# A list scheduler inside the kernel, 4096-wide feed-forward groups, and zeros sent through TensorE during the first keys

## The chip, the core and the metric

The kernel runs on one core of one Trainium2 chip. The metric is the time of one execution in microseconds of device time. The profile's span, from the first to the last instruction, is about 2 us shorter. In the profile's lines PE is TensorE (matrix multiply), PEld its weight loads, DVE is VectorE, ACT is ScalarE, POOL is GpSimd and SP is the engine that issues most DMAs. A run is called slow when it is over 1.5% above the fastest of the same kernel; only fast runs are compared unless the text says otherwise. The sets of experiments ran on four different chips, so each ratio below is to the runs of the kernel before in the same set.

## The reference, cut to what matters

```python
# attention with sketched features: batch 4, heads 4, 1088 positions, head_dim 32, r = 8
a = S1 x ; b = S2 x                       # 8 numbers each per position
phi(x) = outer(a, b)                      # 64 features
kv = sum over s of phi(k) v ; z = sum over s of phi(k)
x = (phi(q) kv) / (phi(q) z + 1e-6)       # 4352 tokens x 128
# feed-forward, d_ff = 2048
h = x @ w_in
P = a0 + a1 h + a2 h^2 + a3 h^3
Q = 1 + |b0| |h| + |b1| h^2
out = (P / (Q + 1e-6)) @ w_out            # float32
```

## The kernel before: what the change and the argument touch

Work is cut into eight chunks of 512 tokens and one of 256. A chunk first needs the keys of its batch (`kv`), then its queries, which give the transposed activations `xT`, and then goes through the feed-forward part. There the 2048 hidden columns of 512 tokens are taken in four groups; a group's tiles are 128 partitions x 2048 elements.

```python
def moe_chunk(xT, W, gf, fill, store_rows):          # gf = 4
    for g in range(ng):
        hb = ...                                      # bf16 copy of h
        for s in range(0, gf, nsub):
            h_ps = hps.tile([128, 1024], FP, name="h_ps")
            ... matmul(h_ps, lhsT=w_in_sb[...], rhs=xT)          # L287
            nc.scalar.copy(out=hb[...], in_=h_ps)                # L289
        m = |hb|                 # bitwise and, VectorE            L291
        u = m * b1 + b0          # VectorE                         L294
        u = u * m                # VectorE                         L296
        L = Ln(u + 1)            # ScalarE                         L298
        r = Exp(-L)              # ScalarE: 1/Q                    L300
        p = hb * a3 + a2         # VectorE                         L302
        p = p * hb               # VectorE                         L304
        p = p + a1               # VectorE                         L305
        p = p * hb               # VectorE                         L306
        y = p * r                # VectorE                         L308
        ... matmul(out_ps, w_out * a0, r), then matmul(out_ps, w_out, y)   # L313
        for f in fill[g::ng]:    # a piece of the next chunk's queries and keys
            f()
# ... cut: key_features, kv_add, query_pieces (p_qT, p_pair(0), p_pair(1), p_xT), output
```

So a group has eight wide VectorE instructions in two chains: the denominator chain (`m`, `u`, `u`, then Ln and Exp on ScalarE) and the numerator chain (four instructions, then the product with `r`). In `p_pair` one pair of heads goes through matmul, ScalarE copy, matmul, VectorE product `q_pT`, matmul `nd`, VectorE division, and only then the second pair starts. The text gives an order of issue, but the framework may move instructions of each engine by its own priorities.

## Time and profile before

| | before |
|---|---|
| time, median of the first 4 runs | 363.36 us (361.62 to 364.05) |
| span of the profiled run | 359.8 us |
| start, until the first `m` on VectorE | 44.43 us |
| middle, first `m` to the end of the last `y` | 307.11 us, VectorE busy 280.65 |
| tail | 8.3 us |

TensorE's busy share is not a good measure of how near it is to its limit: the Trainium skill, "Perfetto Trace Analysis", section "Identifying the Most-Contended Engine", says so, because matmuls are pipelined, and this case agrees, since the same number of recorded matmuls (1004) fills 270 us of the middle here and 248 us in the changed kernel.

Two stretches of the same kernel, from the windows view. The columns are the stretch, its length, and the busy us (and count) of each engine:

```profile
core 0: us, PE busy (x) PEld busy (x) DVE busy (x) ACT busy (x) POOL busy (x), PEclk, DMA share, GB/s
0.00:44.43 44.43, 35.13 (x111) 24.08 (x112) 11.06 (x33) 8.38 (x14) 6.60 (x27) 1.00 0.58 175
44.43:351.54 307.11, 269.98 (x1004) 136.17 (x1020) 280.65 (x379) 219.28 (x195) 2.75 (x2) 0.94 0.03 11
```

In the start VectorE does 11 us of work in 44. In the middle it is idle for 26.5 us. Its largest wait, from the view of its waits (us in total, times, longest), is for `hb`; the longest of the five is the first `m`, so 12.7 us of it fall into the middle:

```profile
DVE m L291 <- ACT hb L289: 20.2, 5, 7.5
```

Four lines from the timeline, start and duration first, show the start of the kernel and, for comparison, the same matmul later:

```profile
22.94 2.07 PE L231 MATMUL w_ps<-qT,Srep_158 64*128 64x512 f32 x2 [0.67 <-ACT qT L225]
29.48 2.07 PE L231 MATMUL w_ps<-qT,Srep_158 64*128 64x512 f32 x2
44.43 0.69 DVE L291 TENSOR_SCALAR m<-hb 128x2048 int16<-128x2048 int16 x1 [7.45 <-ACT hb L289]
46.71 1.12 PE L231 MATMUL w_ps<-qT,Srep_158 64*128 64x512 f32 x2
```

One logical matmul in float32 is recorded as two. It takes 2.07 us at 23 us and 1.12 us at 47 us: TensorE runs at half rate in the start, although the PEclk column says 1.00 there. The Trainium skill, "TensorE: Matmul & The Clock Gate", Part 1, says that an idle array is gated to half rate and released by some 3.4 us of sustained work. The halved duration agrees with the two rates. The release does not come as stated: in the record TensorE works nearly without a gap from 10 to 20 us, and stays at half rate.

```profile
10.00:20.00 10.00, 9.53 (x44) 9.22 (x43) 2.93 (x10) 1.30 (x4) 0.00 (x0) 1.00 0.84 261
12.67 3.20 PE L188 MATMUL kv_ps<-v_aug,k_p 128*128 128x66 f32 x14
```

The same 14 matmuls take 1.78 us at 64.71 us.

Finally the order of VectorE in the middle, from its timeline:

```profile
87.23 1.22 DVE L306 TENSOR_TENSOR p<-p,hb 128x2048 bf16<-128x2048 bf16 x1
88.37 0.81 DVE L294 TENSOR_SCALAR u<-m,b_abs 128x2048 bf16<-128x2048 bf16 x1
89.09 0.81 DVE L302 TENSOR_SCALAR p<-hb,a_sb 128x2048 bf16<-128x2048 bf16 x1
89.81 1.22 DVE L296 TENSOR_TENSOR u<-u,m 128x2048 bf16<-128x2048 bf16 x1
90.95 1.22 DVE L304 TENSOR_TENSOR p<-p,hb 128x2048 bf16<-128x2048 bf16 x1
```

The two chains alternate, so that no instruction needs its neighbour's result. Each starts 0.08 to 0.09 us before the recorded end of the one in front (88.37 + 0.81 = 89.18, the next starts at 89.09).

### The profile page before, as it was taken

How to read it: one execution, taken by the hardware profiler on the slowest of the kernel's cores; microseconds unless marked ns; L12 is line 12 of the kernel's file. 1: busy time of each engine (PE TensorE's matmuls, PEld its weight loads, DVE VectorE, ACT ScalarE, POOL GpSimd, SP SyncE). 2: the span in 40 equal slices, each digit the busy share in tenths (PEclk: the TensorE clock that was granted, in tenths of full speed). 3: DMA queues.
4: the chain of work that ended last, by engine and by line, in shares of the span. 5: the costliest groups of instructions: out<-in, count | busy, mean ns of one | idle time of the engine just before them, and what ended most of it. 6: DMA issues, size and time to landing. Idle time of an engine off the chain costs nothing.

```text
span 359.8 us, 3085 instructions
## 1 busy us (share of the span) xinstructions
PE 307.7 (86%) x1124; PEld 161.5 (45%) x1141; DVE 291.7 (81%) x411; ACT 228.4 (63%) x211; POOL 9.3 (3%) x29
## 2 busy tenths in 40 slices
PE   3988999899869998899598999996899689949652
PEld 2855435654323455544244466443444234426431
DVE  1323199999997998899889998999889984998790
ACT  2110387648947885679649964896499556972960
POOL 4011000030000000000000000000000000000000
PEclk9999999999998999999989999999899959996965
DMA  5791300200000200000000000000000000000000
GB/s 146 240 311 47 118 0 1 60 0 1 29 0 2 87 0 2 1 29 0 2 0 0 29 2 0 29 0 3 0 0 30 0 2 29 0 0 0 2 29 16
DMA packets 12127, 11.22 MB, mean 31 GB/s; under 512 B 4048, under 2 KB 10448, under 8 KB 11984
## 3 DMA queue, kind: packets, MB, share of 16 engines
q1 hardware_dynamic: 12112, 11.02, 9.9%
q8 instruction: 9, 0.15, 0.2%
q14 instruction: 6, 0.05, 0.0%
HBM read 8.79 MB, written 2.23 MB: 31 GB/s over the span
## 4 chain that ended last, share of the span: by engine, by line
PE 55%; DVE 21%; ACT 19%; issue 2%; DMA 1%; SPq 0%; DVEq 0%; ACTq 0%
PE h_ps L287 22%; PE out_ps L313 12%; ACT L L298 8%; PE kv_ps L188 5%; ACT hb L289 5%; PE w_ps L231 4%; DVE y L308 4%; PE w_ps L236 4%; DVE u L296 3%; PE w_ps L243 3%; DVE p L306 3%; DVE p L304 2%; PE w_ps L171 2%; DVE u L294 2%; DVE m L291 2%
## 5 line engine op out<-in xcount | busy, mean ns | idle before, releaser
L287 PE MATMUL h_ps<-xT,w_in_sb 128*128 128x512 f32 (+1 forms) x288 | 137.0, 608 | 4.2 <-ACT xT L260 2.4
L289 ACT CAST hb<-h_ps 128x1024 bf16<-128x1024 f32 x68 | 67.9, 1016 | 42.9 <-PE h_ps L287 42.9
L287 PEld LDWEIGHTS h_ps<-xT,w_in_sb 128*128 128x128 f32 x288 | 55.2, 203 | 60.3 <-issue 38.7
L298 ACT ACTIVATE L<-u,one_ap 128x2048 f32<-128x2048 bf16 x34 | 68.3, 2010 | 8.8 <-DVE u L296 8.6
L313 PE MATMUL out_ps<-y,w_out_b 128*128 128x512 bf16 (+1 forms) x139 | 39.5, 408 | 4.9 <-DVE y L308 4.5
L306 DVE TENSOR_TENSOR p<-p,hb 128x2048 bf16<-128x2048 bf16 x34 | 41.4, 1218 | 0.2
L304 DVE TENSOR_TENSOR p<-p,hb 128x2048 bf16<-128x2048 bf16 x34 | 41.4, 1218 | 0.2
L296 DVE TENSOR_TENSOR u<-u,m 128x2048 bf16<-128x2048 bf16 x34 | 41.3, 1214 | 0.0
L291 DVE TENSOR_SCALAR m<-hb 128x2048 int16<-128x2048 int16 x34 | 23.2, 683 | 20.3 <-ACT hb L289 20.2
L313 PEld LDWEIGHTS <-w_out_a_291 128*128 128x128 bf16 x144 | 14.5, 102 | 42.3 <-issue 34.3
L313 PEld LDWEIGHTS <-w_out_b 128*128 128x128 bf16 x144 | 15.1, 109 | 29.4 <-issue 20.8
L302 DVE TENSOR_SCALAR p<-hb,a_sb 128x2048 bf16<-128x2048 bf16 x34 | 27.3, 804 | 0.0
L294 DVE TENSOR_SCALAR u<-m,b_abs 128x2048 bf16<-128x2048 bf16 x34 | 27.1, 798 | 0.0
L305 DVE TENSOR_SCALAR p<-p,a_sb 128x2048 bf16<-128x2048 bf16 x34 | 26.2, 770 | 0.3
L243 PEld LDWEIGHTS w_ps<-kv_dup,q_pT 128*128 128x128 f32 x128 | 17.4, 208 | 15.4 <-DVE q_pT L239 14.8
L243 PE MATMUL w_ps<-kv_dup,q_pT 128*128 128x66 f32 x128 | 18.9, 296 | 4.7 <-DVE q_pT L239 4.7
L188 PEld LDWEIGHTS kv_ps<-v_aug,k_p 128*128 128x128 f32 x128 | 19.3, 227 | 6.1 <-issue 2.9
L231 PE MATMUL w_ps<-qT,Srep_158 64*128 64x512 f32 (+1 forms) x36 | 21.3, 672 | 0.7 <-ACT qT L225 0.7
L188 PE MATMUL kv_ps<-v_aug,k_p 128*128 128x66 f32 x128 | 20.2, 309 | 0.7 <-DVE k_p L180 0.7
L236 PE MATMUL w_ps<-qT,Srep_162 64*128 64x512 f32 (+1 forms) x36 | 20.2, 643 | 0.3 <-ACT A_sb L234 0.3
L234 ACT COPY A_sb<-w_ps 128x512 f32<-128x512 f32 (+1 forms) x18 | 10.1, 562 | 13.2 <-PE w_ps L231 13.1
L239 DVE TENSOR_TENSOR q_pT<-A_sb,w_ps 128x512 f32<-128x512 f32 (+1 forms) x18 | 11.7, 653 | 7.2 <-PE w_ps L236 7.0
(167 smaller groups left out, 304.1 us busy)
## 6 DMA issues: line engine op xcount, KB each, us to landing
in_k_dram<-in_k_dram SPq DMA_DIRECT2D x4, 512.0 KB, 3.9
in_v_dram<-in_v_dram SPq DMA_DIRECT2D x4, 512.0 KB, 5.2
in_q_dram<-in_q_dram SPq DMA_DIRECT2D x4, 512.0 KB, 4.3
out_dram<-oT SPq DMA_DIRECT2D x8, 256.0 KB, 2.0
w_in_sb<-in_moe_w_in_dram SPq DMA_DIRECT2D x1, 1024.0 KB, 8.3
k_rem<-in_k_dram SPq DMA_DIRECT2D x4, 32.0 KB, 4.1
v_rem<-in_v_dram SPq DMA_DIRECT2D x4, 32.0 KB, 2.2
q_rem<-in_q_dram SPq DMA_DIRECT2D x4, 32.0 KB, 5.8
```

Source lines behind the costliest of these rows:

```text
L188: nc.tensor.matmul(kv_tiles[b][:, hp * 66:(hp + 1) * 66], lhsT=k_rows[:, hp * 128:(hp + 1) * 128], rhs=v_rows[:, 2 * hp:2 * hp + 2, :], st ...
L231: nc.tensor.matmul(A_ps[:, :W], lhsT=Srep[0][rows].rearrange("p g f -> p (g f)"), rhs=st["qT"][rows, :W], start=True, stop=True)
L236: nc.tensor.matmul(B_ps[:, :W], lhsT=Srep[1][rows].rearrange("p g f -> p (g f)"), rhs=st["qT"][rows, :W], start=True, stop=True)
L243: nc.tensor.matmul(nd_ps[r0:r1, i * 66:(i + 1) * 66], lhsT=q_pT[:, i * 128 + r0:i * 128 + r1], rhs=kv_of(b, i, hp), start=True, stop=True)
L287: nc.tensor.matmul(h_ps[:, i * W:(i + 1) * W], lhsT=w_in_sb[:, fi * 128:(fi + 1) * 128], rhs=xT[:, :W], start=True, stop=True)
L289: nc.scalar.copy(out=hb[:, s * W:(s + nsub) * W], in_=h_ps)
L294: nc.vector.tensor_scalar(out=u[:, :GW], in0=m[:, :GW], scalar1=b_abs[:, 1:2], scalar2=b_abs[:, 0:1], op0=AX.mult, op1=AX.add)
L296: nc.vector.tensor_mul(out=u[:, :GW], in0=u[:, :GW], in1=m[:, :GW])
L298: nc.scalar.activation(out=L[:, :GW], in_=u[:, :GW], func=ACT.Ln, bias=one_ap)
L304: nc.vector.tensor_mul(out=p[:, :GW], in0=p[:, :GW], in1=hb[:, :GW])
L306: nc.vector.tensor_mul(out=p[:, :GW], in0=p[:, :GW], in1=hb[:, :GW])
L313: nc.tensor.matmul(out_ps[:, :W], lhsT=W_terms[t][:, fi, :], rhs=ys[t][:, i * W:(i + 1) * W], start=(g == 0 and t == 0 and i == 0), stop=( ...
```

## The change

The intent is to feed VectorE without gaps: decide the order of every engine's queue in the kernel, halve the number of wide VectorE instructions, and raise TensorE's clock early. The long diff is cut to its core.

```diff
+class Plan:                       # every step: engine, estimated ns, what it follows, rank, buffers taken and given
+    HOP = 190
+    def issue(self):
+        while todo:                # of the steps that are ready, the one that can start first, then by rank
+            ...
+            key = (t, s["rank"], s["n"])
+        for s in sorted(done, key=lambda s: (s["start"], s["n"])):
+            s["fn"]()
-    GF = 4
+    GF = 8                        # groups of 4096 elements
+    LW = 2048                     # Ln and Exp stay 2048 wide
+    FR = 1.45                     # feed-forward matmuls ranked 1.45 groups ahead
+    FIRST = [4, 4, 8]             # group sizes of the first chunk
+    LAST = [8, 4, 4]              # and of the last, 256-token chunk (2048, 1024, 1024)
+    ctx.enter_context(tc.manual_schedule())
+    BUFS = dict(xT=3, hb=3, m=1, u=2, r=2, y=2, L=2, h_ps=2, ...)
+    def warm(n):
+        for _ in range(n):
+            nc.tensor.matmul(warm_ps[0], lhsT=zeros[:, :128], rhs=zeros, start=True, stop=True)
+    # warm(8) first; then 1 or 2 of them among the transposes, projections and kv
+    # matmuls of the first keys, and in the first chunk's queries
+    c_w = plan.add("DVE", 2500, weights, after=[ld["ab"], ld["wo"]], rank=-0.25, give=["L"])
+    # queries: both pairs of heads advance together, step by step, instead of one after the other
+    d1 = plan.add("DVE", ts, d_abs, after=[he, c_b], rank=g - 0.5, take=["m"])
+    d2 = plan.add("DVE", ts + 100, d_lin, after=[d1], rank=g - 0.5, take=["u"])
+    d3 = plan.add("DVE", tt, d_mul, after=[d2], rank=g - 0.5, give=["m"])
+    ... Ln, Exp and the r half of the projection, 2048 columns at a time ...
+    p = plan.add("DVE", ts + 100, n_first, after=[he, ld["ab"]], rank=g - 0.3, take=["y"])
+    p = plan.add("DVE", tt, n_mul, after=[p], rank=g - 0.3)
+    p = plan.add("DVE", ts + 50, n_add, after=[p], rank=g - 0.3)
+    p = plan.add("DVE", tt, n_mul, after=[p], rank=g - 0.3, give=["hb"])
+    p = plan.add("DVE", tt, n_over, after=[p, e], rank=g + 0.55)
# ... cut: all helpers turned into steps; the numerator is now formed in y, without a tile p
```

## The prediction

> **What bounds the kernel now.** The span is 359.8 us (median time 364.03). Windows view, three stages:
>
> 1. Start, 0 to 44.4 us: VectorE is nearly empty (about 11 us busy); it waits 7.5 us for the first `hb`. The timeline shows one serial chain (keys, `kv`, queries, `xT`, first `h_ps`), with the PE clock low: a pair of `L231` matmuls takes 2.07 us here and 1.05 us later; the first `h_ps` pair about 1.7 us against 0.86 us later (the granted-clock row's 1.0 contradicts that). The Trainium skill, "TensorE: Matmul & The Clock Gate", Part 1, says an idle array runs at half rate until about 3.4 us of sustained work; the halved durations agree.
> 2. Middle, 44.4 to 351.6 us (307.2 us): VectorE busy 280.7 us (91%), ACT 219, PE about 270 by the record, but by full-clock spacings (0.86 us per `h_ps` matmul, 0.22 us per `out_ps` matmul) I estimate 250 us of real PE work. VectorE is the bound; 26 us of idle remain.
> 3. Tail, 8.3 us from the last `y` to the end.
>
> **What the change does.**
>
> - Zeros through PE: 8 matmuls before the keys and some 30 among them, at 0.22 us warm about 7 us of extra PE work. If the clock rises, the pre-`h_ps` chain halves in its PE parts. By hand: `kv` ready about 17.5 us (was 22.5), `xT` about 25 (was 38.3), first VectorE group instruction about 30 us instead of 44.4. Gain 14 us.
> - 4096-wide groups: 34 groups become 20, about 112 fewer wide VectorE instructions. At 77 to 187 ns of start cost each that looks like 12 us; I expect almost none. In before, instructions of two chains alternate (`m`, `p`, `u`, `p`, ...) and start 0.61, 0.72, 1.14 us apart although they last 0.68, 0.81, 1.22: independent neighbours overlap. Where neighbours depend on each other (the last group), the starts are 0.85 and 1.25 us apart. The new order runs each chain straight through (`m`,`u`,`u`; then `y`,`y`,`y`,`y`), five of eight instructions dependent, costing 0.11 us each. Per 4096 columns: before 2 x 7.28 = 14.56 us, after about 14.27. The whole is about 247 us either way. Ln and Exp stay 2048 wide.
> - Scheduler order: orders come from durations close to the trace's, and feed-forward matmuls are hoisted 1.45 groups ahead. VectorE efficiency in the middle should rise from 91% to about 96.5%: (247 + 32 of small operations)/0.965 = 289 us, a gain of 18 us.
> - Tail: last group 1024 wide, 4 matmuls instead of 8: about 7.5 us.
>
> **Sum.** 30 + 289 + 7.5 = 326.5 us span; time about 2 us over the span, as before: **328 us**, 8 in 10 between 315 and 344. Faster by over 2%: 0.95; within 2%: 0.04; slower: 0.01.
>
> **What would show each step right or wrong.** First `m` at 27 to 34 us, and early `w_ps` pairs near 1.05 us rather than 2 us; wide VectorE instructions averaging about 1.22, 1.33 and 2.29 us, total VectorE busy near 285 to 292, hardly down; VectorE idle in the middle below 15 us; PE clock dips rarer; tail 7 to 8 us.
>
> **What would make it wrong.** The zeros may fail to raise or hold the clock between the short matmuls (start 35 to 40 us). The fixed order stalls an in-order engine where real times differ from the planned ones (up to 345). Dependent neighbours may cost less at 4096 (down to 318).

## More of the kernel before

From the page of the kernel before, the busy times of the engines and the chain that ended last (the chain of waits), by engine and then by line:

```profile
PE 307.7 (86%) x1124; PEld 161.5 (45%) x1141; DVE 291.7 (81%) x411; ACT 228.4 (63%) x211; POOL 9.3 (3%) x29
PE 55%; DVE 21%; ACT 19%; issue 2%; DMA 1%; SPq 0%; DVEq 0%; ACTq 0%
PE h_ps L287 22%; PE out_ps L313 12%; ACT L L298 8%; PE kv_ps L188 5%; ACT hb L289 5%; PE w_ps L231 4%; DVE y L308 4%; PE w_ps L236 4%; DVE u L296 3%; PE w_ps L243 3%; DVE p L306 3%; DVE p L304 2%; PE w_ps L171 2%; DVE u L294 2%; DVE m L291 2%
```

No engine owns the chain: it passes between PE, VectorE and ScalarE.

## The result, and the profile after

The changed kernel takes 324.28 us (median of 4 runs, 323.23 to 326.02) against 363.36 us. The ratio of the fast runs is 0.8936, with a 95% interval from 0.8882 to 0.8990. Such a ratio is the mean time of one kernel's fast runs over that of the other's fast runs of the same rounds, so it is not quite the ratio of the medians. The result is correct. The profiled run has a span of 323.9 us.

The same parts of the page after the change:

```profile
PE 280.0 (86%) x1153; PEld 150.0 (46%) x1172; DVE 286.5 (88%) x300; ACT 228.4 (71%) x213; POOL 8.7 (3%) x29
DVE 77%; PE 13%; DMA 5%; issue 1%; SPq 1%; ACT 1%; DVEq 0%
DVE y L503 22%; DVE u L486 11%; DVE y L510 10%; DVE y L499 6%; DVE u L482 6%; DVE y L506 6%; PE h_ps L466 6%; DVE m L476 5%; DMA L<-in_moe_w_out_dram 3%; DVE q_pT L398 3%; DVE k_p L314 2%; PE out_ps L517 2%; PE w_ps L405 2%; DMA v_sb<-in_v_dram 2%; PE w_ps L389 2%; DVE x_sb L417 2%
```

VectorE's work hardly fell (291.7 to 286.5 us) although it has 111 instructions fewer. What changed is who owns the chain: VectorE, with 77% in place of 21%. The windows view of the two stretches:

```profile
0.00:35.77 35.77, 30.78 (x144) 18.84 (x147) 11.36 (x34) 9.55 (x16) 6.62 (x27) 0.95 0.74 217
35.77:316.47 280.70, 247.57 (x1004) 130.46 (x1020) 275.15 (x267) 218.07 (x195) 2.09 (x2) 0.97 0.04 12
```

The profiled runs are the fastest of the four before and the slowest of the four after, so their spans differ by less than the medians (39.1 us). The 35.9 us between the spans are 8.7 us in the start (44.43 to 35.77), 26.4 us in the middle (307.11 to 280.70) and 0.8 us in the tail (8.26 to 7.43). Of the 26.4 us, 5.5 are less VectorE work and 20.9 less VectorE idle time (26.5 to 5.6). The wait for `hb` is left at the first `m` alone:

```profile
DVE m L476 <- ACT hb L472: 7.5, 1, 7.5
```

VectorE's order in the middle, after:

```profile
219.71 1.22 DVE L476 TENSOR_SCALAR m<-hb 128x4096 int16<-128x4096 int16 x1
220.97 1.34 DVE L482 TENSOR_SCALAR u<-m,b_abs 128x4096 bf16<-128x4096 bf16 x1
222.35 2.29 DVE L486 TENSOR_TENSOR u<-u,m 128x4096 bf16<-128x4096 bf16 x1
224.56 2.29 DVE L510 TENSOR_TENSOR y<-y,r 128x4096 bf16<-128x4096 bf16 x1
226.76 1.34 DVE L499 TENSOR_SCALAR y<-hb,a_sb 128x4096 bf16<-128x4096 bf16 x1
228.14 2.29 DVE L503 TENSOR_TENSOR y<-y,hb 128x4096 bf16<-128x4096 bf16 x1
```

Each chain now runs straight through. Where an instruction needs its neighbour's result it starts 0.04 us after the neighbour's end (219.71 + 1.22 = 220.93, next 220.97); where it does not (224.56 after 222.35 + 2.29 = 224.64), 0.08 us before. So a dependence costs 0.12 us here, and a group has five.

The start did not go as predicted. From the timeline after the change, VectorE and then TensorE:

```profile
20.54 1.29 DVE L258 TENSOR_SCALAR w_out_108<-L,a_sb 128x2048 bf16<-128x2048 f32 x1 [2.27 <-DMA L<-in_moe_w_out_dram]
21.75 1.22 DVE L259 CAST w_out_109<-L 128x2048 bf16<-128x2048 f32 x1
23.00 1.29 DVE L398 TENSOR_TENSOR q_pT<-A_sb,w_ps 128x512 f32<-128x512 f32 x2
35.77 0.69 DVE L476 TENSOR_SCALAR m<-hb 128x2048 int16<-128x2048 int16 x1 [7.49 <-ACT hb L472]
23.74 1.18 PE L405 MATMUL w_ps<-kv_dup,q_pT 128*128 128x66 f32 x8 [2.71 <-DVE q_pT L398]
25.57 1.81 PE L405 MATMUL w_ps<-kv_dup,q_pT 128*128 128x66 f32 x8
```

The two conversions of `w_out` stand in VectorE's queue in front of the first `q_pT`. They wait for their load, and TensorE waits 2.71 us behind them. After that gap its second set of `L405` matmuls takes 1.81 us. Up to the gap the start had gone as predicted: `kv` was ready at 16.96 us (17.5 predicted), and two early pairs of `w_ps` matmuls took 1.87 us together.

### The profile page after: what moved, and what is told of

It reads as the page before. It is cut to its first block, busy times and chain, and to the rows that moved or that the text cites. A ratio compares the mean times of both kernels' runs of the same rounds, so it can differ in the third digit from the quotient of the medians.

```text
span 323.9 us, 3027 instructions
## 1 busy us (share of the span) xinstructions
PE 280.0 (86%) x1153; PEld 150.0 (46%) x1172; DVE 286.5 (88%) x300; ACT 228.4 (71%) x213; POOL 8.7 (3%) x29
## 4 chain that ended last, share of the span: by engine, by line
DVE 77%; PE 13%; DMA 5%; issue 1%; SPq 1%; ACT 1%; DVEq 0%
DVE y L503 22%; DVE u L486 11%; DVE y L510 10%; DVE y L499 6%; DVE u L482 6%; DVE y L506 6%; PE h_ps L466 6%; DVE m L476 5%; DMA L<-in_moe_w_out_dram 3%; DVE q_pT L398 3%; DVE k_p L314 2%; PE out_ps L517 2%; PE w_ps L405 2%; DMA v_sb<-in_v_dram 2%; PE w_ps L389 2%; DVE x_sb L417 2%
## 5 line engine op out<-in xcount | busy, mean ns | idle before, releaser
L490 ACT ACTIVATE L<-u,one_ap 128x2048 f32<-128x2048 bf16 (+1 forms) x35 | 68.4, 1954 | 18.1 <-DVE u L486 18.1
L503 DVE TENSOR_TENSOR y<-y,hb 128x4096 bf16<-128x4096 bf16 (+2 forms) x40 | 78.9, 1972 | 1.2
L495 ACT ACTIVATE r<-L 128x2048 bf16<-128x2048 f32 (+1 forms) x35 | 65.4, 1870 | 0.4
L517 PE MATMUL out_ps<-r,w_out_108 128*128 128x512 bf16 (+1 forms) x139 | 35.6, 378 | 11.6 <-ACT r L495 11.2
L517 PE MATMUL out_ps<-y,w_out_109 128*128 128x512 bf16 (+1 forms) x132 | 34.4, 389 | 10.7 <-DVE y L510 9.9
L486 DVE TENSOR_TENSOR u<-u,m 128x4096 bf16<-128x4096 bf16 (+2 forms) x20 | 39.4, 1971 | 0.6
L510 DVE TENSOR_TENSOR y<-y,r 128x4096 bf16<-128x4096 bf16 (+2 forms) x20 | 39.3, 1965 | 0.1
L517 PEld LDWEIGHTS <-w_out_109 128*128 128x128 bf16 x144 | 14.4, 104 | 32.1 <-issue 21.7
L482 DVE TENSOR_SCALAR u<-m,b_abs 128x4096 bf16<-128x4096 bf16 (+2 forms) x20 | 23.7, 1185 | 0.6
L499 DVE TENSOR_SCALAR y<-hb,a_sb 128x4096 bf16<-128x4096 bf16 (+2 forms) x20 | 23.6, 1181 | 0.0
L405 PE MATMUL w_ps<-kv_dup,q_pT 128*128 128x66 f32 x128 | 16.9, 288 | 5.4 <-DVE q_pT L398 5.4
L405 PEld LDWEIGHTS w_ps<-kv_dup,q_pT 128*128 128x128 f32 x128 | 16.6, 204 | 9.7 <-DVE q_pT L398 7.7
L389 PE MATMUL w_ps<-qT,Srep_106 64*128 64x512 f32 (+1 forms) x36 | 16.9, 615 | 0.1
```

What stands on the lines that cost most here:

```text
L405: nc.tensor.matmul(nd_ps[r0:r1, i * 66:(i + 1) * 66], lhsT=T["q_pT", n, hp][:, i * 128 + r0:i * 128 + r1], rhs=kv_of(b, i, hp), start=True ...
L482: nc.vector.tensor_scalar(out=T["u", g][:, :gw], in0=T["m", g][:, :gw], scalar1=b_abs[:, 1:2], scalar2=b_abs[:, 0:1], op0=AX.mult, op1=AX.add)
L486: nc.vector.tensor_mul(out=T["u", g][:, :gw], in0=T["u", g][:, :gw], in1=T["m", g][:, :gw])
L490: nc.scalar.activation(out=T["L", g, l0][:, :lw], in_=T["u", g][:, l0:l0 + lw], func=ACT.Ln, bias=one_ap)
L495: nc.scalar.activation(out=T["r", g][:, l0:l0 + lw], in_=T["L", g, l0][:, :lw], func=ACT.Exp, scale=-1.0)
L499: nc.vector.tensor_scalar(out=T["y", g][:, :gw], in0=T["hb", g][:, :gw], scalar1=a_sb[:, 3:4], scalar2=a_sb[:, 2:3], op0=AX.mult, op1=AX.add)
```

## The experiments

All kernels gave correct results. The first `m` and the last `y` of each are read from its timeline, the busy times between them from its windows view.

| kernel | time, median us | ratio to before | first `m` | middle | VectorE busy in it |
|---|---|---|---|---|---|
| before | 363.36 | | 44.43 | 307.11 | 280.65 |
| changed | 324.28 | 0.894 | 35.77 | 280.70 | 275.15 |
| no_zeros | 331.14 | 0.914 | 42.82 | 282.29 | 275.36 |
| narrow | 356.92 | 0.982 | 38.17 | 309.60 | 295.19 |
| narrow_alt | 331.22 | 0.919 | 36.50 | 285.26 | 281.08 |
| before_wide | 450.58 | 1.244 | 48.88 | 390.77 | 267.73 |
| framework_order | 328.18 | 0.906 | 40.22 | 278.90 | 266.69 |
| weights_late | 320.47 | 0.882 | 31.38 | 279.55 | 274.96 |
| alternate | 324.46 | 0.892 | (slow profile) | | |
| both | 321.89 | 0.885 | 33.41 | 279.09 | 268.01 |
| lagged | 343.68 | 0.948 | (slow profile) | | |
| lagged_fr | 332.50 | 0.918 | 33.23 | 289.92 | 269.85 |
| before_zeros | 372.43 | 1.017 | (slow profile) | | |

The medians in the table include slow runs, where there were any; the ratios do not, and each is to the runs of the kernel before in its own rounds.

### 1. Is it the zeros that shorten the start? (no_zeros)

```diff
-        for _ in range(n):
+        for _ in range(0):
             nc.tensor.matmul(warm_ps[0], lhsT=zeros[:, :128], rhs=zeros, start=True, stop=True)
```

> The changed kernel, same order of every other instruction, but no zeros are sent through PE. If the zeros are what raises the clock in the start (my theory), the early transposes, kv and L389 matmuls run at half rate, kv is ready about 5 us later than 17 us, the first m comes at 40 to 43 us instead of 35.8, and the time is about 330 us (326 to 333). Rival: the start is held by the w_out load (VectorE waits for it until 20.5 us), so the zeros are hidden and the time stays within 1.5 us of 324.3.

Measured: 331.14 us, first `m` at 42.82 us, the middle nearly unchanged (282.29 us). The theory held and the rival fell. The zeros are worth about 7 us, all of it in the start: they are most of the gain of the start (7.05 of 8.66 us). From TensorE's timeline, the `kv` matmuls of the changed kernel and then of no_zeros, 0.145 and 0.227 us each:

```profile
10.21 1.16 PE L328 MATMUL kv_ps<-v_aug,k_p 128*128 128x66 f32 x8
```

```profile
10.72 3.63 PE L328 MATMUL kv_ps<-v_aug,k_p 128*128 128x66 f32 x16
```

The zeros are matmuls of 512 columns, put between short ones. The short ones alone keep TensorE nearly as busy in the record, but do not raise its clock; the runs do not show why. The `kv` result was only 3.4 us later (20.31 for 16.96 us), not 5; the rest was lost in the query and the first `h_ps` matmuls, which ran at the low clock too.

### 2. Zeros put into the kernel before (before_zeros)

```diff
+    def warm(n, rhs):
+        for _ in range(n if warm_on[0] else 0):
+            nc.tensor.matmul(warm_ps[:, :rhs.shape[1]], lhsT=zeros, rhs=rhs, start=True, stop=True)
# 16 times before the keys, then after the first keys' and first query's matmuls, with their own data as rhs
```

> The kernel before with matmuls by zero weights before and among the first keys and the first query, tied to the data there so that the framework keeps them in place; nothing else changed. My theory: early L231-like pairs fall from 2.07 to about 1.1 us, first m at 36 to 40 us instead of 44.4, time 356 to 360 us. Rival: the zeros take as much as they give, 362 to 366 us.

Measured: fast runs 368.5 us, 1.7% slower (95% interval of the ratio 1.0096 to 1.0242, the recorded verdict is unclear), so neither theory held as written. It is not a clean test. Tying the zeros to the data, so that the framework keeps them in place, made them float32, each recorded as two matmuls, so they cost more than the bfloat16 zeros of the changed kernel. In the profiled run (slow) the clock did rise for a while: an early `L231`-like pair took 1.12 us in place of 2.07. But the padding delayed the keys, and the first `m` came at 53.27 us. It shows that padding costs when it stands in the way; it says nothing on bfloat16 zeros in the kernel before.

### 3. Width under the old order (before_wide)

```diff
-    GF = 4
+    GF = 8
+    LW = 2048
# Ln and Exp in two halves; numerator formed in y; one m, two r, one o_sb buffer (as in the changed kernel);
-            for f in fill[g::ng]:
+            for f in [f for i, f in enumerate(fill) if (i % 4) // (4 // ng) == g]:
```

> The kernel before with groups of 4096, Ln and Exp still 2048 wide, numerator formed in y, buffers as in the changed kernel, order left to the framework. My theory: the framework alternates the two chains, so VectorE work falls by 0.88 us per 4096 columns, 15 us in all (busy about 277 us), but its idle time in the middle (26 us) stays or grows, and the first m waits 4 us longer for its wider hb: 348 us (342 to 358). Rival: width is the whole gain: 325 to 332.

Measured: 450.58 us, far outside both expectations. VectorE's work fell as expected, to 267.73 us in the middle, but its idle time there grew to 123 us. These are the longest waits of VectorE and of TensorE in that kernel (us in total, times, longest):

```profile
DVE m L292 <- ACT hb L290: 75.2, 9, 11.9
DVE y L309 <- ACT r L302: 35.0, 13, 2.9
PE w_ps L244 <- DVE q_pT L240: 62.9, 18, 8.0
```

One of the waits of TensorE, in the timeline of ScalarE, VectorE and TensorE:

```profile
114.18 0.58 ACT L235 COPY A_sb<-w_ps 128x512 f32<-128x512 f32 x1
119.27 2.28 DVE L306 TENSOR_TENSOR y<-y,hb 128x4096 bf16<-128x4096 bf16 x1
121.47 2.28 DVE L297 TENSOR_TENSOR u<-u,m 128x4096 bf16<-128x4096 bf16 x1
123.67 1.28 DVE L307 TENSOR_SCALAR y<-y,a_sb 128x4096 bf16<-128x4096 bf16 x1
124.87 0.68 DVE L240 TENSOR_TENSOR q_pT<-A_sb,w_ps 128x512 f32<-128x512 f32 x1
125.60 1.97 PE L244 MATMUL w_ps<-kv_dup,q_pT 128*128 128x66 f32 x8 [7.96 <-DVE q_pT L240]
```

A 0.68 us product, whose input `A_sb` was done at 114.76 us, stands behind wide instructions in VectorE's queue until 124.87; TensorE, also in order, does nothing for 7.96 us, and `h_ps` matmuls behind it come late, which starves VectorE in turn. The Trainium skill, "TensorE: Matmul & The Clock Gate", calls the queues of ScalarE and VectorE strict FIFO (the table at its head) and says that matmuls stay in program order (Part 2); the lines agree. "Perfetto Trace Analysis", section "Optimizing Scalar/DVE Operations", says that grouping into larger operations can help throughput if the engine is saturated, and that breaking up may help where VectorE is not saturated but holds up others. The second half is seen here: VectorE is busy for 62% of the span, and the narrower groups of the kernel before are 87 us faster. Under the list scheduler the same width goes with 324 us.

The run also has fewer buffers of `m` (one for two) and `r` (two for three) than the kernel before, and its pieces of the next chunk stand elsewhere. No run separates these from the width; the waits shown are for data, not for a free buffer.

### 4. Width under the new order (narrow, narrow_alt)

```diff
# narrow: the changed kernel with
-    GF = 8 ; FR = 1.45 ; FIRST = [4, 4, 8] ; dict(..., hb=3, m=1, u=2, r=2, y=2, ...) ; rank = first_of[n] - 2.6
+    GF = 4 ; FR = 2.9 ; FIRST = [4, 4, 4, 4] ; dict(..., hb=6, m=2, u=4, r=4, y=4, ...) ; rank = first_of[n] - 5.2
# narrow_alt: the same, and the chains interleaved
+        d1 = m ; p1 = first numerator step after d1 ; d2 after p1 ; p2 after d2 ; d3 after p2 ; p3 after d3 ; last n_mul after p3
```

> The changed kernel with groups of 2048 (last two of the last chunk still 1024), ranks and buffer counts doubled so that the lookahead in columns is the same. My theory: with chains run straight through, a 2048-wide group costs VectorE 7.87 us, so width is worth 2 x 7.87 - 14.27 = 1.47 us per 4096 columns, 22 us in all: VectorE busy about 290 us plus more gaps, time about 345 us (338 to 350). Rival 1: width is worth only the 0.88 us that independent neighbours show: about 337. Rival 2: the list scheduler alone made the gain, width nothing: 324 to 327.

> The list scheduler with 2048-wide groups (as narrow) and the two chains of a group interleaved (as alternate), so that VectorE has the same work as in the kernel before, about 290 us busy, and only the order of issue and the start differ from it. If the order by itself takes idle time out of the middle, the stretch from the first m to the last y falls from 307 us to 290 to 297 us and the time is 334 to 342 us. Rival: the order pays only together with wide groups, and the stretch stays at 303 us or more: 347 us or more.

Measured: narrow 356.92 us, narrow_alt 331.22 us. Against the kernel before, the recorded verdict of both is unclear; the 95% interval of the ratio is 0.9735 to 0.9896 for narrow and 0.9075 to 0.9306 for narrow_alt. The middle of narrow and then of narrow_alt, from their windows views:

```profile
38.17:347.77 309.60, 268.68 (x1021) 137.90 (x1020) 295.19 (x387) 221.08 (x195) 1.54 (x2) 0.90 0.03 11
```

```profile
36.50:321.76 285.26, 255.69 (x1021) 132.43 (x1020) 281.08 (x387) 219.73 (x195) 1.12 (x2) 0.95 0.03 12
```

Narrow was expected at 345 us and took 12 us more. The busy figure of 290 us in the expectation was a slip: 22 us more than the changed kernel's 286.5 is 308.5, and 306.5 was measured over the span. The rest of the miss is idle time, 14.4 us in the middle, partly the 0.04 us behind each dependent neighbour, partly waits for the queries' matmuls. The two kernels differ in the order of the chains, from which the scheduler places the rest anew, so at 2048 columns the straight order costs 24.3 us of middle, 14.1 of them as busy time. Five dependences in each of the 33 groups of 2048, at 0.12 us, make an estimate of 20 us of this. The granted clock also differs (0.90 and 0.95), and its share is not separated.

Narrow_alt is the cleanest test of the schedule: VectorE has nearly the same groups, the same width and the same work as in the kernel before (281.08 and 280.65 us), and the middle is 21.9 us shorter. One rival stands untested: narrow_alt also has more buffers than the kernel before (`hb` six for three, `u` four for two, `r` four for three, `y` four for two `y` and two `p`, `xT` three for two), and both pairs of heads advance together in it. No run gives the old order these buffers at this width. Before_wide had as many bytes of `hb` and `u` buffers under the old order and was slow, so these alone do not feed VectorE at 4096 columns. So "order of issue" below means the list scheduler's order with the buffers and the query order that it was given. It did somewhat better than expected (285.26 for 290 to 297 us). Its rival, that the order pays only with wide groups, fell.

### 5. Is the manual schedule needed? (framework_order)

```diff
-    ctx.enter_context(tc.manual_schedule())
```

> The changed kernel with the line that turns the manual schedule on taken out: the same instructions, buffers and order of issue by the list scheduler, but the framework may reorder each engine's queue by its own priorities. It alternates the two VectorE chains, so VectorE busy should be about 277 to 280 us. If the fixed order is what keeps VectorE fed (my theory, after the 450 us of wide groups under the framework's order), waits for hb and r come back and the time is 345 us or more. Rival: the order of issue alone carries the gain and the framework keeps it: 318 to 330.

Measured: 328.18 us. My theory fell and the rival held. The framework did reorder, with the chains alternating again in most places, and the middle was as good as with the fixed order:

```profile
40.22:319.12 278.90, 248.88 (x1021) 129.70 (x1020) 266.69 (x267) 216.87 (x195) 1.10 (x2) 0.97 0.04 12
```

What carries the middle is the order in which the list scheduler issues the steps, not the ban on moving them. The ban is worth about 4 us in the start. Without it the framework moved most of the zeros, which nothing ties to other work, in front of everything else on TensorE:

```profile
1.19 8.90 PE L220 MATMUL out_ps<-zeros 128*128 128x512 bf16 x28 [1.19 <-DVE zeros L226]
```

So the first use of the sketch tile waited 9.2 us in place of 4.4. From the view of VectorE's waits (us in total, times, longest), first of the changed kernel, then of framework_order:

```profile
DVE sT L237 <- PE w_ps L234: 4.4, 1, 4.4
```

```profile
DVE sT L236 <- PE w_ps L233: 9.2, 1, 9.2
```

### 6. What made the first `m` late? (after_again, weights_late)

```diff
-    c_w = plan.add("DVE", 2500, weights, after=[ld["ab"], ld["wo"]], rank=-0.25, give=["L"])
# ... and after the first chunk's queries have been added:
+    c_w = plan.add("DVE", 2500, weights, after=[ld["ab"], ld["wo"], x_steps[0]], rank=-0.25, give=["L"])
```

> The changed kernel once more, as the control on the chip of the next three runs: 323 to 326 us.

> The changed kernel, but the two conversions of w_out are put on VectorE after the first chunk's division instead of before its q_pT products, so that nothing in the first query waits for the w_out load. If that wait is why the first m came at 35.8 us and not at 30 (my theory), q_pT starts at about 20.3 instead of 23.0 us, PE has no gap of 2.7 us there, its clock stays up, the first m comes at 30 to 32 us, and the time is 318 to 321 us. Rival: the w_in load or the cold h_ps matmuls hold the first hb anyway: m at 35 us, time within 1.5 us of the control.

The control gave 323.41 and 324.32 us in its fast runs, and 328.52 and 333.3 in two slow ones. Weights_late gave 320.41 to 322.45 us and no slow run. My theory held: the first `q_pT` came at 20.27 us and the first `m` at 31.38. The clock column of the windows view, third from the right, tells why; two lines of the changed kernel, then two of weights_late:

```profile
20.00:24.00 4.00, 1.29 (x5) 0.47 (x5) 3.42 (x4) 0.00 (x0) 0.00 (x0) 1.00 1.09 323
24.00:28.00 4.00, 3.78 (x19) 2.96 (x19) 1.59 (x7) 0.00 (x0) 1.14 (x2) 0.58 0.88 259
```

```profile
20.00:24.00 4.00, 3.96 (x24) 2.57 (x24) 2.67 (x8) 0.00 (x0) 0.00 (x0) 1.00 1.06 306
24.00:28.00 4.00, 3.91 (x12) 1.44 (x12) 3.55 (x3) 1.76 (x3) 1.67 (x2) 1.00 0.80 224
```

The gap on TensorE is gone, and with it the drop of the clock to 0.58. The durations agree with this column: the second set of the same matmuls took 1.00 us in place of 1.81. The conversions run later, in time in which VectorE has nothing else to do. This is the fastest kernel: by the means of the fast runs 2.9 us (0.9%) below the control, by the medians 3.8 us below the changed kernel. That is a small difference, but the ranges of their fast runs do not meet.

### 7. Are dependent neighbours worth removing at 4096? (alternate, both, lagged, lagged_fr)

```diff
# alternate: m, y=first, u, y*hb, u*m, y+a1, y*hb in this order (as in narrow_alt); both: alternate and weights_late
# lagged: weights_late, with the numerator steps of group g-1 between the denominator steps of group g
# lagged_fr: lagged with
-    FR = 1.45
+    FR = 2.1
```

> The changed kernel with the two VectorE chains of a group interleaved (m, y, u, y, u, y, ..., y), everything else as it was; the scheduler places the rest again. My theory of dependent neighbours: starts come 0.11 us earlier at five places of each group, 0.59 us per 4096 columns, so VectorE busy falls from 286.5 to about 275 us and the time to 312 to 316 us. Rival 1: the order of the chains costs VectorE nothing: busy 284 or more, time 323 to 326. Rival 2: busy falls as I say, but Ln starts 4 us later in each group and VectorE then waits for r: time 318 or more.

> weights_late and alternate together: the gains are in different stages and should add, 307 to 312 us. If alternate alone does nothing, as weights_late.

> weights_late, with the numerator chain of a group interleaved with the denominator chain of the next group, so that VectorE's neighbours are independent without Ln starting later than its place and with only two y tiles alive. If alternate failed because Ln came late and because a third y was wanted, VectorE busy is about 279 us here and its waits in the middle stay near those of weights_late: 312 to 316 us. Rival: with VectorE at 279 us the next bound is already PE and ACT with their buffers, any order gives 319 to 323.

> lagged with the feed-forward matmuls hoisted 2.1 groups ahead instead of 1.45, since a group's hb is now wanted earlier. If the waits that are left are for hb, 2 to 4 us less than lagged; if they are for r or the queries, no gain or a loss of some us.

Measured: alternate 323.4 to 324.5 us in its fast runs, both 321.89, lagged 343.68, lagged_fr 332.50. None beats weights_late. The work did fall as the theory of dependent neighbours says; these are the middles of weights_late and of both:

```profile
31.38:310.93 279.55, 249.97 (x1021) 130.60 (x1020) 274.96 (x267) 217.88 (x195) 2.09 (x2) 0.96 0.04 12
```

```profile
33.41:312.50 279.09, 251.72 (x1021) 134.40 (x1020) 268.01 (x267) 218.88 (x195) 3.35 (x2) 0.95 0.03 12
```

VectorE has 7.0 us less to do and the middle is 0.5 us shorter: the rest came back as waits after the first `m`: 4.4 us for `r`, 2.6 for the queries' matmuls and 1.8 for `hb`. This is the second rival of alternate, in part: busy time fell, and the waits ate it. Moving the numerator one group later (lagged) was meant to avoid late Ln and did worse: even with more lookahead (lagged_fr) VectorE waited 16.0 us for `hb` after the first `m` (20.8 less 4.8), where weights_late has no such wait, as a group's `hb` was then wanted before TensorE had it. Lookahead helped lagged by 10 us (means of the fast runs), more than the 2 to 4 expected.

## Why the prediction was right, point by point

The time, 328 us predicted and 324.28 measured, lay well inside the range. Two terms of the sum were off in opposite directions, the start by 5.8 us and the middle by 8.3, and partly cancelled; that the sum came as near as 4 us is luck.

- **The start, 30 us predicted, 35.77 measured.** This term was mis-sized. The mechanism of the zeros was right (no_zeros: 7 us lost without them), but the hand-made time line left out that the list scheduler had put the two `w_out` conversions, 2.5 us, in front of the first `q_pT`, and that their load would hold them until 20.5 us. The order of VectorE's instructions could have been read from the changed kernel before predicting. Moving these two instructions gave 31.38 us. The prediction's test for the clock held: early `w_ps` pairs took 0.93 to 1.12 us and not 2.
- **The middle, 289 us predicted, 280.70 measured.** The direction was right and the size too small. The prediction said VectorE would be about 96.5% efficient, a figure for which it gives no working; VectorE was busy 98.0% of the middle (275.15 of 280.70). Its work was predicted to stay, and fell by 5.5 us. Narrow_alt shows that the order of issue, with the buffers it was given, is worth 21.9 us at unchanged work and width; from there to the changed kernel, width and straight chains together are worth another 4.6 us (285.26 to 280.70).
- **Width together with straight chains saves VectorE almost nothing: right for this kernel.** The prediction said that straight chains would give back what width saves. The four combinations under the new order show it as busy time in the middle: 281.08 us (2048, alternating), 295.19 (2048, straight), 275.15 (4096, straight), 268.01 (4096, alternating, in both). At a fixed order of the chains width saves 13 to 20 us of VectorE's work. The step from the first to the third, which the change takes, is only 5.9 us. Mean durations were 1.22, 1.34 and 2.29 us, as predicted.
- **"VectorE is the bound" of the kernel before** was too simple. By the estimate above it had the largest busy share, but the chain of waits gave it 21%, TensorE 55% and ScalarE 19%. Much of its idle time came from the exchange between in-order queues, which before_wide shows at its worst. Were VectorE's work alone the bound, before_wide, which has 13 us less of it in the middle, should have been faster.
- **The fixed order.** The prediction named order as the source of the middle's gain without telling the list scheduler's order of issue from the fixed schedule. Framework_order tells them apart: the first carries the middle, the second only about 4 us in the start.
- **The tail** was 7.4 us (7.5 predicted), and VectorE's idle time in the middle 5.6 us (below 15 predicted). The clock granted in the middle rose from 0.94 to 0.97, as "dips rarer" said.

What stays open: the middle is 279 to 282 us in five kernels whose VectorE is busy between 267 and 275 us in it (the changed one, weights_late, both, framework_order, no_zeros). So something besides VectorE's work seems to hold it there. The waits of `both` point to the supply of `hb`, `r` and the query matmuls, and a third `y` buffer was not tried; no run separates these. Nor does a run separate the list scheduler's order from the deeper buffers and the joint advance of the two pairs of heads.

## What to carry to other kernels

When several in-order engines feed each other, look at who owns the chain of waits before making the busiest engine's instructions cheaper: here wider instructions under the old order cost 24%, a better order of issue (with more buffers) took 22 us out of the middle at the old width, and only with that order did the width do no harm. Cheaper instructions and instructions that need their neighbour's result can cancel; count both from starts, not durations. When a list scheduler places one-off preparation, check what stands behind it in the queue: two conversions waiting for a load cost 3 to 4 us here and let TensorE's clock drop.

## What the Trainium skill lacked or had wrong

- "VectorE: DVE Perf Modes", section "The DRAIN you can't avoid", says that the next operation does not start until the pipe is empty, and then points to a model, on the same page, of when one starts earlier. Neither has a figure for what a dependence costs. Here wide neighbours without a dependence start 0.08 to 0.09 us before the recorded end of the one in front, and dependent ones 0.04 us after it. That is about 0.12 us for each dependence, by estimate some 20 of the 24.3 us of the middle between narrow and narrow_alt.
- "TensorE: Matmul & The Clock Gate", Part 1, speaks of idle windows of about 3.4 us, and its section "Why this matters for your kernels" advises no gaps above some 3 us. In the changed kernel a gap of 2.71 us, with mostly short matmuls behind it, was followed by a clock of 0.58 over 24 to 28 us; with the gap taken out it stayed at 1.00.
- The same page does not say which matmuls count as sustained work. In the kernel before, short ones of 64 to 128 columns kept TensorE busy for 9.53 us between 10 and 20 us and did not raise the clock: 14 of them took 3.20 us there and 1.78 us later. Nor does it say whether matmuls of all-zero operands raise it. They do: without them the first `m` came 7 us later and the time grew from 324.28 to 331.14 us.
- The same page warns that recorded clock events are not to be trusted one by one, but not that the clock as profiled can be wrong from the first instruction on: the PEclk column says 1.00 in the start of the kernel before, where a matmul pair takes 2.07 us in place of 1.12.
- "Perfetto Trace Analysis", section "Optimizing Scalar/DVE Operations", has the right advice on grouping and breaking up, but no size for the harm: 450.58 us in place of 363 us when groups were widened and short products stood behind 2.28 us instructions.
